# A gated linear attention and a squared-relu MLP on one core: block products in digit order, and a planner with new durations, a margin and new priorities

## The chip, the cores and the metric

The kernel runs on one core of a Trainium2 chip. The metric is the device time of one execution in microseconds; lower is better. A core has five engines that run side by side, each through its own list of instructions in a fixed order: TensorE (PE, with its weight loads PEld), VectorE (DVE), ScalarE (ACT), GpSimd (POOL) and SyncE (SP). SP and POOL here mostly issue DMA transfers. An instruction that isn't ready holds up everything behind it on its engine, whether that is ready or not.

## The reference

Four batches of 768 tokens, eight heads of 48 features. Each head has a complex state that decays by a per-token, per-feature factor and takes in k times v; the query reads its real part. The result is laid out as 3072 tokens by 384 features and goes through an MLP with 2048 hidden features.

```python
mag = np.sqrt(a_re * a_re + a_im * a_im)
scale = np.minimum(mag, 0.999) / (mag + 1e-06)
a_re_n, a_im_n = (a_re * scale, a_im * scale)
...
    new_re = ar * S_re - ai * S_im
    new_im = ar * S_im + ai * S_re
    kv = np.einsum('bhd,bhe->bhde', k[:, :, t], v[:, :, t])
...
h = x @ w_in
r = np.maximum(h, 0.0)
return (r * r @ w_out).astype(np.float32)
```

Here `kv` is the outer product of k and v of the token, added to `new_re`; the output is q times the real state.

## The kernel before

**Units.** The 3072 tokens are cut into six units of 512 (`NU` = 6). In a unit, a row of SBUF holds four neighbouring tokens, so that there are 128 groups of four. Each unit goes through three stages:

- `load` and `chain`: SP loads a, q, k and v. ACT and DVE normalise the decays (`roots`, `normalise`), multiply them up within each group of four (`inner`) and invert them (`inverse`). Then the running complex product over the 128 groups is formed. `totals` transposes the groups' totals on PE, so that features lie on partitions and groups along the row; ACT copies them into the tile `e`. `scan` forms the running product on DVE in three levels, each with a block of four or eight: within blocks of four groups, within blocks of four of those (tile `inc`), over the rest (tile `top`), and then back down. Each complex product in `product` is three DVE instructions (lines 989, 991, 993). The tile `x` takes a simpler real scan (line 963). `back` transposes the results on PE again (line 922), ACT copies them to `xn` (line 1055), and `apply` multiplies them into q and k on DVE (lines 1086 to 1104).
- `pairs`: per pair of heads, q and k are transposed, by PE and ACT in the first two units (`turn_pe`, lines 1186 and 1189) and by DVE and DMA later (`turn`, lines 1163 and 1167, into tiles `QT`). PE forms scores (line 1203), DVE masks them (line 1206), the states are kept (lines 1219 to 1237), and PE mixes (lines 1249 and 1253). ACT copies the result (line 1259) and SP moves it into `xT` (line 1267). `xT` has two slots, for even and odd units.
- `dense`: in two groups of 256 tokens, PE multiplies by w1 (line 1296), ACT applies relu and square (lines 1303 and 1304), PE multiplies by w2 (line 1314), ACT copies out (line 1318) and SP stores (line 1323). Twelve such groups in all.

**Weights.** They come as 64-bit words in sixteen pieces (`fetch` on POOL, line 728) and are converted by one ACT and three DVE instructions (`convert`, lines 738 to 747). The raw words are parked in tiles that are needed for other things later: raw w1 in the place of w2, in the g tiles and in a v tile; raw w2 in w2's free places, the v tile and the three QT tiles. So `pairs` of unit 1 has to wait for w2's raw words to leave QT. At the end `inspect` reads the weights once more and a check decides whether a general path has to run.

**Order.** The order isn't written out: every piece of work is entered as a step with an engine, an estimated duration, reads, writes and a rank. The class `Plan` then simulates the engines: it takes the engine that can start soonest and on it, among the steps that are ready at that time, the one of lowest rank. A step counts as ready after its inputs' ends plus `HOP` of their engine. The instructions are emitted in the order of the simulated start times, and that order is fixed on each engine on the chip. Ranks are pairs, compared left to right: pairs (1, unit), chain (2, unit), dense and weight conversion (3, ...), inspection (5, ...).

```python
def tt(n):
    return n / 960.0 + 0.07
...
CHAIN, PAIR, DENSE, CONV, LATE = 2, 1, 3, 3, 5
```

`tt`, `ts2` and `ac` estimate DVE, DVE fast forms and ACT from the elements per row; `dma` gives an issue time, a latency and a share of a bus.

## Time and profile before

| | us |
|---|---|
| median of 3 runs | 849.73 (849.67 to 854.43) |
| profiled execution, its own time | 850.27 |
| its span, first to last instruction | 848.5 |
| PE busy | 680.8 (80%) |
| PE weight loads busy | 517.5 (61%) |
| DVE busy | 516.5 (61%) |
| ACT busy | 339.3 (40%) |
| POOL busy | 78.2 (9%) |
| dense matmuls, line 1296, 1152 of 391 ns each | 268.6 |
| dense matmuls, line 1314, 768 of 494 ns each | 260.0 |

Matmuls overlap, so the sums by line run above the time that they take up: in the last 165 us a dense group takes 41.4. The page has a picture of the span in 40 slices of 21.2 us, each digit being the busy share in tenths, and PEclk the clock that TensorE was granted, in tenths of full speed:

```profile
PE   0117743199988999979879898987899999999994
DVE  5998899955588977799259995779656100000000
ACT  6632764133783435720088234661023131322220
PEclk9999977599999999989899999998899999999998
DMA  9803760372130266205490055501799200000001
```

DVE is nearly full in the first 200 us, in which the first two units' chains and the weights' conversion fall. PE is nearly full from there on, with dips at each unit's chain. From about 670 us only dense work is left and DVE is done.

### The profile page before, as it was taken

Reading aid. Unit: us, or ns where it says so; the run is one execution under the profiler, and the core shown is the slowest. Engines: PE = TensorE matmul, PEld = TensorE weight load, DVE = VectorE, ACT = ScalarE, POOL = GpSimd, SP = SyncE. Lnnn points to the kernel's source line nnn. Section 1 sums busy time; section 2 is a strip of 40 time slices with the busy share of each in tenths; the row PEclk is TensorE's granted clock in tenths of the full one; section 3 lists DMA queues with packets and bytes.
Section 4 is the critical chain, followed back from the end, with each engine's and each line's share of the span. In section 5 each row is a group of like instructions: output and inputs, shape, how many; then the busy total and the mean of one; then the engine's idle time right before and its main releaser. Section 6 shows DMA issues by size and latency. Waiting matters only on the chain.

```text
span 848.5 us, 10163 instructions
## 1 busy us (share of the span) xinstructions
PE 680.8 (80%) x3566; PEld 517.5 (61%) x3566; DVE 516.5 (61%) x978; ACT 339.3 (40%) x577; POOL 78.2 (9%) x154
## 2 busy tenths in 40 slices
PE   0117743199988999979879898987899999999994
PEld 0007633175875886756766596675687777777772
DVE  5998899955588977799259995779656100000000
ACT  6632764133783435720088234661023131322220
POOL 4000100010000220007000050003312000000000
PEclk9999977599999999989899999998899999999998
DMA  9803760372130266205490055501799200000001
GB/s 298 258 0 87 207 118 0 88 229 47 31 54 10 75 163 176 45 1 147 116 186 18 20 121 133 148 10 36 188 270 319 63 0 19 1 19 1 19 0 24
DMA packets 80509, 79.43 MB, mean 94 GB/s; under 512 B 35776, under 2 KB 65216, under 8 KB 80448
## 3 DMA queue, kind: packets, MB, share of 16 engines
q1 hardware_dynamic: 71488, 48.40, 23.7%
q0 software_dynamic: 8960, 30.29, 11.7%
q8 instruction: 30, 0.49, 0.3%
q14 instruction: 31, 0.25, 0.1%
HBM read 48.76 MB, written 4.72 MB: 63 GB/s over the span
## 4 chain that ended last, share of the span: by engine, by line
PE 42%; DVE 27%; SPq 8%; DMA 8%; ACT 6%; issue 4%; DVEq 0%; ACTq 0%; POOLq 0%
PE d L1314 18%; PE d L1296 17%; SPq L1167 5%; PE sc L1203 3%; DVE f L989 3%; DVE f L991 2%; DVE f L863 2%; DVE e L993 2%; DMA aq<-in_a_im_dram 2%; DMA QT<-aq 2%; DVE f L1091 2%; DVE f L1102 2%; DMA xT<-yt 1%; PE tr L1219 1%; DVE w L747 1%
## 5 line engine op out<-in xcount | busy, mean ns | idle before, releaser
L1296 PE MATMUL d<-xT,w 128*128 128x256 f32 x1152 | 268.6, 391 | 26.0 <-ACT g L1303 8.0
L1296 PEld LDWEIGHTS d<-xT,w 128*128 128x128 f32 x1152 | 222.7, 196 | 64.5 <-ACT g L1303 10.0
L1314 PE MATMUL d<-w,g 128*128 128x384 f32 x768 | 260.0, 494 | 1.5 <-DVE w L747 1.5
L1314 PEld LDWEIGHTS d<-w,g 128*128 128x128 f32 x768 | 146.0, 193 | 97.4 <-issue 4.5
L1303 ACT ACTIVATE g<-d 128x512 f32<-128x512 f32 x96 | 57.1, 595 | 138.0 <-PE d L1296 115.9
L1341 DVE TENSOR_SCALAR flag<-tr 1x1 int32<-1x1 f32 x1 | 0.1, 145 | 174.0 <-PE tr L1340 174.0
L1127 POOL DMA_DIRECT2D KC<-f x104 | 50.9, 498 | 375.8 <-DVE f L1102 188.1
L1203 PE MATMUL sc<-QT 96*128 96x128 f32 x384 | 52.2, 285 | 15.5 <-DMA QT<-aq 14.7
L1304 ACT ACTIVATE g<-g 128x512 f32<-128x512 f32 x96 | 60.6, 631 | 3.1
L1203 PEld LDWEIGHTS sc<-QT 96*128 96x128 f32 x384 | 48.6, 196 | 20.5 <-issue 15.4
L1318 ACT COPY ot<-d 128x384 f32<-128x384 f32 x24 | 11.5, 477 | 123.4 <-PE d L1314 120.2
L1206 DVE TENSOR_TENSOR A<-sc,mask 128x512 f32<-128x512 f32 x48 | 32.4, 686 | 39.8 <-PE sc L1203 39.8
L922 PE MATMUL tr<-ident,xn 128*128 128x128 f32 x54 | 10.3, 306 | 43.0 <-ACT xn L894 39.7
L1259 ACT COPY yt<-yp 112x512 f32<-112x512 f32 x24 | 13.9, 579 | 74.7 <-PE yp L1253 69.1
L1102 DVE TENSOR_TENSOR f<-aq 128x768 f32<-128x768 f32 x48 | 42.9, 954 | 0.4
L922 PE MATMUL tr<-ident,e 128*128 128x128 f32 x36 | 9.2, 427 | 42.1 <-DVE e L993 42.1
L1091 DVE TENSOR_TENSOR f<-aq,xn 128x768 f32<-128x768 f32 x48 | 42.5, 949 | 0.0
L1249 PE MATMUL yp<-A,v 128*48 128x128 f32 x384 | 37.8, 285 | 2.7 <-ACT yt L1259 2.0
L863 DVE TENSOR_TENSOR f<-aq 128x384 f32<-128x384 f32 x72 | 37.0, 555 | 1.0
L922 PEld LDWEIGHTS tr<-ident,xn 128*128 128x128 f32 x54 | 6.8, 152 | 46.7 <-issue 29.1
L1219 PEld LDWEIGHTS tr<-v,KC 128*96 128x96 f32 x320 | 31.9, 178 | 3.6 <-DMA xT<-yt 2.0
L922 PEld LDWEIGHTS tr<-ident,e 128*128 128x128 f32 x36 | 6.8, 218 | 44.6 <-DVE e L993 44.6
(143 smaller groups left out, 789.0 us busy)
## 6 DMA issues: line engine op xcount, KB each, us to landing
QT<-aq SPq DMA_DIRECT2D x192, 64.0 KB, 2.3
f<-in_moe_w_in_dram POOLq DMA_DIRECT2D x8, 768.0 KB, 8.8
f<-in_moe_w_out_dram POOLq DMA_DIRECT2D x8, 768.0 KB, 7.1
KC<-f POOLq DMA_DIRECT2D x104, 48.0 KB, 2.2
v<-in_v_dram SPq DMA_DIRECT2D x96, 48.0 KB, 2.5
out_dram<-ot SPq DMA_DIRECT2D x96, 48.0 KB, 1.6
xT<-yt SPq DMA_DIRECT2D x36, 96.0 KB, 3.7
aq<-in_a_re_dram SPq DMA_DIRECT2D x8, 384.0 KB, 3.8
```

Of the source, the lines that this page charges most:

```text
L863: dve.tensor_tensor(out=f, in0=a[:, :, :, c - 1], in1=a[:, j, :, c].unsqueeze(1).to_broadcast([C, 2, HH, D]), op=ALU.mult)
L1091: lambda j=j, f=f, r=r: dve.tensor_tensor(out=f[:, r], in0=a[:, r], in1=over(j), op=ALU.mult), rank)
L1102: lambda j=j, r=r, o=o: dve.tensor_tensor(out=o[:, :, :, r * D:(r + 1) * D], in0=qk[:, j], in1=a[:, r], op=ALU.mult), rank)
L1127: lambda i=i, c=c: queue.dma_start(out=kc[32 * c:32 * c + 32, i], in_=nat[32 * i:32 * i + 32, c]),
L1167: lambda b=b, j=j, z=z, t=t, T6=T6: sp.dma_start(out=t[32 * j:32 * j + 32, b], in_=T6[32 * b:32 * b + 32, i % 2, j]), rank, 65536,
L1203: pe.matmul(sa[:, j], lhsT=T[:, j, 1, h], rhs=T[:, j, 0, h], start=True, stop=True)
L1219: pe.matmul(ps[:, j, h], lhsT=kc[:, j, (2 * i + h) % HH], rhs=v5[:, j, 2 * i + h], start=True, stop=True)
L1249: pe.matmul(ypair[64 * h:64 * h + D, ts(j, C)], lhsT=v5[:, j, 2 * i + h], rhs=aa[h][:, j], start=True, stop=at[j] is None)
L1296: pe.matmul(ps[:, j], lhsT=w1[:, f // FP, m, ts(f % FP, C)], rhs=xT[:, m, base:base + G], start=(m == 0), stop=(m == NM - 1))
L1303: act.activation(out=o, in_=ps, func=AF.Relu)
L1304: act.activation(out=o, in_=o, func=AF.Square)
L1314: pe.matmul(ps, lhsT=gt[:, f % 2, ts(i, C)], rhs=w2[:, f], start=(f == 0), stop=(f == NF - 1))
```

## The change

It has five parts.

1. **Layout of the block products.** The 128 groups' index is read as three digits (k of 8, x of 4, w of 4). `e` is now laid out with w outermost, then x, then the feature block m and k; `inc` with x outermost. Every operand of a product of one level is then a run without gaps. To get there, `totals` transposes with a permutation matrix `perm` in place of the identity for the two complex parts, and writes PSUM in runs of eight (`spread`). The permutation also shifts by one group, so that ACT's copy to `e` is one run. `perm` is made by three POOL copies at the start. In `back` a new ACT copy per part puts `e` back into natural order before the transposes.
2. **Durations.** `HOP`, `ts2`, `ac`, the DMA issue time and latency and several steps' durations have other values.
3. **Margin.** In the plan, after 100 us, a PE step that depends on another engine or a DMA counts as ready 1.0 us later.
4. **Relu and output copy.** Their ACT steps have rank (0, unit): ahead of all others.
5. **Weight conversion.** w1's conversions have rank (2.5, piece), w2's (2, 0.6): behind the chain of unit 0, ahead of that of unit 1. The fetches keep their rank.

```diff
@@ -481,7 +481,8 @@
 class Plan:
 
 
-    HOP = {"PE": 0.12, "DVE": 0.1, "ACT": 0.15, "POOL": 0.2, "SP": 0.05}
+    HOP = {"PE": 0.3, "DVE": 0.17, "ACT": 0.1, "POOL": 0.2, "SP": 0.05}
+    MARGIN = 1.0
     RATE = 280e3
 
     def __init__(self):
@@ -530,7 +531,10 @@
             t = 0.0
             for d in steps[n][2]:
                 same = steps[d][0] == e and steps[d][5] is None
-                t = max(t, done[d] + (0.0 if same else self.HOP[steps[d][0]]))
+                hop = 0.0 if same else self.HOP[steps[d][0]]
+                if e == "PE" and not same and done[d] > 100.0:
+                    hop += self.MARGIN
+                t = max(t, done[d] + hop)
             at[n] = t
             wait[e].append(n)
 
...
@@ -653,6 +658,12 @@
     ypair = bank["yp"]
 
     make_identity(nc, ident)
+
+    turn_ = As[0][:, 0:C]
+    pool.tensor_copy(out=turn_[:, 1:C], in_=ident[:, 0:C - 1])
+    pool.tensor_copy(out=turn_[:, 0:1], in_=ident[:, C - 1:C])
+    pool.tensor_copy(out=perm.rearrange("p (w x k) -> p k x w", w=4, x=4),
+                     in_=turn_.rearrange("p (k x w) -> p k x w", w=4, x=4))
     pool.memset(mask, 1.0)
     for c in range(W):
         rows = mask[32 * c:32 * c + 32]
...
@@ -673,19 +684,20 @@
         return n / 960.0 + 0.07
 
     def ts2(n):
-        return n / 1920.0 + 0.08
+        return n / 1920.0 + 0.18
 
     def ac(n):
-        return n / 1200.0 + 0.12
+        return n / 1200.0 + 0.18
 
     def step(eng, dur, reads, writes, fn, rank, wire=None, group=None):
         return plan.add(eng, dur, reads, writes, fn, rank, wire, group)
 
-    def dma(q, reads, writes, fn, rank, size, lat=1.6, group=None):
-        step("SP" if q is sp else "POOL", 0.52 if q is sp else 0.8,
+    def dma(q, reads, writes, fn, rank, size, lat=1.8, group=None):
+        step("SP" if q is sp else "POOL", 0.6 if q is sp else 0.7,
              reads, writes, fn, rank, (lat, size), group)
 
     CHAIN, PAIR, DENSE, CONV, LATE = 2, 1, 3, 3, 5
+    W1, W2 = 2.5, 2
 
 
 
...
-        rank = (CONV, i)
+        rank = (W2, 0.6) if i >= NPIECE else (W1, i)
...
-        def turned(j, src, keys, name):
+        def turned(src, put, by, keys):
-            ps = bank[b][:, 0:DM].rearrange("p (m t) -> p m t", m=NM)
-                    pe.transpose(ps[:, m], src(m), ident)
+                    pe.transpose(put(bank[b][:, 0:DM], m), src(m), by)
             step("PE", 0.36, keys, [(b,)], go, rank)
-            return ps, (b,)
+            return bank[b][:, 0:DM], (b,)
+
+        def natural(t, m):
+            return t[:, ts(m, C)]
+
+        def spread(t, m):
+            return t.rearrange("p (y m k) -> p m y k", m=NM, k=8)[:, m]
 
...
-            ps, b = turned(j, lambda m: xn[:, j, ts(m, C)],
-                           [("xn", j, 0), ("xn", j, 1)], "tot")
+            keys = [("xn", j, 0), ("xn", j, 1)]
+            ps, b = turned(lambda m: xn[:, j, ts(m, C)], natural if j == 2 else spread,
+                           ident if j == 2 else perm, keys)
             if j < 2:
+                p4 = ps.rearrange("p (w g) -> p w g", w=4)
+                last = ps.rearrange("p (y m k) -> p y m k", m=NM, k=8)[:, 0, :, 0]
                 step("ACT", ac(DM), [b], [("e", j)], lambda: act.copy(
-                    out=e[:, j, :, 1:C], in_=ps[:, :, 0:C - 1]), rank)
+                    out=e[:, j], in_=p4), rank)
...
                     first = SCALE if j == 0 else 0.0
+                    head = e[:, j, 0].rearrange("p (x m k) -> p x m k", x=4, m=NM)[:, 0]
                     if fresh:
-                        dve.memset(e[:, j, :, 0], first)
+                        dve.memset(head[:, :, 0], first)
                     else:
-                        dve.tensor_copy(out=e[:, j, :, 0], in_=ce[:, j])
+                        dve.tensor_copy(out=head[:, :, 0], in_=ce[:, j])
                     if cross:
-                        dve.memset(e[:, j, :, CUT], first)
+                        dve.memset(head[:, :, 4], first)
...
-            v4 = e.rearrange("p r m (g w) -> p r (m g) w", w=4)
             for w in range(1, 4):
-                product(v4[:, 0:2, :, w], v4[:, 0:2, :, w - 1],
-                        lambda lo, hi, w=w: v4[:, lo:hi, :, w], 192, E, E)
-            i4 = inc.rearrange("p r (k w) -> p r k w", w=4)
+                product(e[:, 0:2, w], e[:, 0:2, w - 1], lambda lo, hi, w=w: e[:, lo:hi, w],
+                        192, E, E)
+            i4 = inc.rearrange("p r (x g) -> p r x g", x=4)
...
-                product(i4[:, 0:2, :, w], i4[:, 0:2, :, w - 1],
-                        lambda lo, hi, w=w: i4[:, lo:hi, :, w], 48, I, I)
+                product(i4[:, 0:2, w], i4[:, 0:2, w - 1], lambda lo, hi, w=w: i4[:, lo:hi, w],
+                        48, I, I)
...
-            x4 = incx.rearrange("p r (k w) -> p r k w", w=4)
-            product(x4[:, 0:2, :, 1:4], i4[:, 0:2, :, 0:3],
-                    lambda lo, hi: tx[:, lo:hi].unsqueeze(3).to_broadcast(
-                        [C, hi - lo, 24, 3]), 144, I, I)
+            step("DVE", 0.16, I, I, shift, rank)
+            x4 = incx.rearrange("p r (x g) -> p r x g", x=4)
+            product(x4[:, 0:2, 1:4], i4[:, 0:2, 0:3],
+                    lambda lo, hi: tx[:, lo:hi].unsqueeze(2).to_broadcast(
+                        [C, hi - lo, 3, 24]), 144, I, I)
...
-            product(v4[:, 0:2], v4[:, 0:2],
-                    lambda lo, hi: incx[:, lo:hi].unsqueeze(3).to_broadcast(
-                        [C, hi - lo, 96, 4]), 768, E + I, E)
+            step("DVE", 0.36, I, I, finish_inc, rank)
+            product(e[:, 0:2], e[:, 0:2],
+                    lambda lo, hi: incx[:, lo:hi].unsqueeze(2).to_broadcast(
+                        [C, hi - lo, 4, 96]), 768, E + I, E)
...
-            ps, b = turned(j, lambda m: x[:, m, 0:C] if j == 2 else e[:, j, m],
-                           [("x",) if j == 2 else ("e", j)], "bk")
+            if j == 2:
+                src, keys = (lambda m: x[:, m, 0:C]), [("x",)]
+            else:
+                line, keys = ff[0][:, Z + j * Y:Z + j * Y + DM], key(0, 2 + j)
+                step("ACT", ac(DM) + 0.2, [("e", j)], keys, lambda: act.copy(
+                    out=line.rearrange("p (g x w) -> p w x g", x=4, w=4),
+                    in_=e[:, j].rearrange("p w (x g) -> p w x g", x=4)), rank)
+                src = lambda m: line[:, ts(m, C)]
+            ps, b = turned(src, natural, ident, keys)
             step("ACT", ac(DM), [b], [("xn", j, 0), ("xn", j, 1)], lambda: act.copy(
-                out=xn[:, j], in_=ps.rearrange("p m t -> p (m t)")), rank)
+                out=xn[:, j], in_=ps), rank)
...
-            step("ACT", 2 * ac(2 * G), [(b, "x"), (b,)], [(b,), ("g", s)], relu, rank)
+            step("ACT", 2 * ac(2 * G), [(b, "x"), (b,)], [(b,), ("g", s)], relu, (0, n))
...
             step("ACT", ac(DM), [(b,)], [("ot", o)], lambda ps=ps, o=o: act.copy(
-                out=ots[o], in_=ps), rank)
+                out=ots[o], in_=ps), (0, n))
```

Left out are lines that carry the layout through (el, sums_of, tops, the last product) and the changed durations of single steps: inner +0.13, the scan of x 2.0 to 2.3, sums_of 0.45 to 0.5, tops 0.2 to 0.33, the sign change 0.09 to 0.12, shift 0.14 to 0.16, finish_inc 0.27 to 0.36, the state sums +0.04 each.

## The prediction

> **What bounds the kernel now.** I read the engine totals first, then TensorE's busy time by stage, then the waits on TensorE, then the order of instructions around the longest of them.
>
> ```profile
> 0.00:100.00 100.00, 33.08 (x282) 28.94 (x282) 84.22 (x161) 54.39 (x88) 11.16 (x30) 1.00 0.56 164
> 100.00:180.00 80.00, 36.39 (x170) 28.65 (x170) 73.20 (x140) 34.15 (x61) 3.52 (x5) 0.72 0.42 105
> 180.00:672.00 492.00, 446.50 (x2481) 339.26 (x2480) 358.89 (x677) 207.58 (x357) 63.57 (x120) 0.96 0.42 107
> 672.00:836.80 164.80, 164.80 (x639) 120.69 (x637) 0.00 (x0) 42.73 (x72) 0.00 (x0) 1.00 0.04 10
> 836.80:848.50 11.70, 0.01 (x1) 0.00 (x0) 0.14 (x1) 0.45 (x1) 0.00 (x0) 0.72 0.12 26
> ```
>
> The columns are stretch, length, busy time of PE, PE weight load, DVE, ACT and POOL, then granted clock. At 672 us DVE is finished and four dense groups are left, which PE does without a gap. So dense work is in stock from about 180 us to the end. What PE loses from there on is not for want of work. It is its own fixed order: it stands at an instruction that isn't ready while ready ones are queued behind. The idle of PE is 66.9 us before 100, 43.6 in 100 to 180, 45.5 in 180 to 672, and 11.7 at the end. The time is PE's work plus these four.
>
> ```profile
> PE tr L922 <- DVE e L993: 42.1, 6, 13.4
> PE sc L1203 <- DMA QT<-aq: 14.7, 12, 3.5
> PE d L1296 <- ACT g L1303: 8.0, 5, 3.1
> PE d L1296 <- DVE w L747: 7.8, 1, 7.8
> ACT QT L1189 <- DVE w L747: 8.2, 1, 8.2
> SPq L1323 <- ACT ot L1318: 235.3, 19, 29.2
> ```
>
> These are the waits: total, times, longest. Adding the single gaps of PE's timeline after 180 us gives: transposes of e on DVE's last product, 15.8 (3.59, 3.93, 3.88 and 4.36 in units 2 to 5); scores on the QT transfers, 14.7; dense matmuls on relu or on the output copy, 9.5; transposes of xn and x, 3.9; w, 1.5. The sum is 45.4, all of that stage.
>
> ```profile
> 372.27 1.54 PE L922 MATMUL tr<-ident,e 128*128 128x128 f32 x6 [3.93 <-DVE e L993]
> 373.60 4.86 PE L1296 MATMUL d<-xT,w 128*128 128x256 f32 x12
> 373.00:374.00 1.00, 1.00 (x5) 0.94 (x4) 1.00 (x2) 0.63 (x2) 0.00 (x0) 0.50 0.00 0
> 378.00:380.00 2.00, 2.00 (x9) 1.29 (x8) 1.97 (x3) 1.23 (x2) 0.00 (x0) 1.00 0.00 0
> ```
>
> The wait costs more than its length: after it the granted clock is 0.50, and twelve dense matmuls take 4.65 us before the next group starts, where the tail does 96 in 20.72 (2.59 for twelve).
>
> **The change part by part.**
>
> *Contiguous products.*
>
> ```profile
> L989 DVE TENSOR_TENSOR f<-e 128x192 f32<-128x192 f32 x18 | 9.0, 503 | 0.3
> L867 DVE TENSOR_TENSOR aq<-f 128x192 f32<-128x192 f32 x36 | 12.9, 358 | 1.2
> L989 DVE TENSOR_TENSOR f<-inc 128x48 f32<-128x48 f32 x18 | 4.4, 242 | 0.4
> ```
>
> The first and third read every fourth element, the second reads runs. Nine products of 192 per unit lose about 0.14 us each, nine of 48 about 0.035: 1.55 us per unit, 9.3 over six units.[...] In unit 1 the scan took 13.06 us (134.05 to 147.11 in the timeline), so about 11.5 after. This shortens DVE's chain, which doesn't set the end: four groups, 165 us, stand behind it.
>
> *The price of the layout.* Each unit gets two ACT copies that scatter e back. Row L1055 has a plain 128x384 copy at 476 ns; were ACT to lose on spread elements what DVE loses, 0.78. I take 0.65, so 7.8 us of ACT in all. Old path from scan to both xn copies in unit 3: 372.25 to 374.33, 2.1 us; new: 0.65 twice, transposes, copy, hops, 2.6. DVE has the two L1086 products and two of L1091 first and asks for the second xn only 3.9 us after the scan, so that hides it. If TensorE comes a dense step later (1.3), it is just met; without that cover DVE stalls about 1 us per unit, again in front of 165 us of stock.
>
> Six transposes per unit now write PSUM in runs of 8. In the trace the contiguous ones are 273 ns, pitch 0.137 (six in 0.82), and no PE row has a spread destination. Here a rule speaks against the change: the Trainium skill, "PSUM — Partial Sum Buffer", Specifications, says that any non-contiguous access pattern slows matmuls significantly. By the row the 36 transposes cost nothing more; by the rule, were it a doubling, 36 x 0.137 = 4.9 us. I take 0, because a run of 8 is nearer to the contiguous row, and keep 0 to 5; a gain is excluded. The three POOL copies at the start, near the 0.2 us memsets there, fall in POOL's idle time before the gate at 5.58.
>
> *Durations and margin.* The planner's old sum for unit 1's scan is 8.69 us (three products of 192 at 0.81, three of 48 at 0.36, the rest as in the code), 4.37 less than measured: that is the 3.6 to 4.4 us by which PE arrives early. With the new figures the plan has 9.04 for an actual 11.5: short by 2.5. The longer hop takes 0.07, the margin 1.0, leaving about 1.4 in each of four units: idle 15.8 to 5.6, gain 10.2.
>
> The slow clock goes with it. Excess over the normal pace after the four waits: 1.4, 2.8, 1.8, 2.0 (for unit 3: transposes 1.54 against 0.82, dense 4.65 against 2.59), sum 7.9. The Trainium skill, "TensorE: Matmul & The Clock Gate", What's actually happening, says that an idle window of some 3.4 us halves the clock and about as much activity restores it. By that rule each wait costs half of 3.4, 6.8 for four; I use the measured 7.9. More important, a gap of 1.4 lies below it, so I expect the whole 7.9 back.
>
> Waits of scores on QT: eleven of twelve are 0.45 to 1.47 us, one is 3.5. Margin 1.0, 0.2 more latency and 0.08 more for each of the DMA issues ahead cover the eleven and a part of the other: gain 12. The score runs at most one dense step later; queued behind it are DVE's mask products, which have idle time there (39.8 us behind scores). xn and x: 3 of 3.9.
>
> *Relu and output copy first on ACT.* The pair is 0.60 + 0.63 us and may now precede a ready chain step of 0.8 to 1.5. In 434 to 444 us PE waited 1.5, 3.1 and 0.6 behind chain work on ACT. Waits on an ACT that itself stands at a DMA stay. Gain 5 of 9.5, w another 1. The chain is pushed back by 1.2 us per collision, again in front of the stock. An earlier output copy frees SP earlier: its four stores (0.6 each) hold SP's queue, with QT transfers and loads behind them, but they are issued where the plan puts them.
>
> *w2 conversion ahead of the next chain.* One is an ACT step (0.89) and three DVE instructions, 0.55 + 0.96 + 0.96 = 2.47 us, and its end frees a slot for a POOL fetch of 768 KB (0.72 to issue, 7 to land), so two fetches move into 95 to 105 us, where the DMA share is already about 1 with chain 1's loads and xT on SP: at 300 GB/s some 5 us. Seven of the eight can go between 92 and 118 us: 17.3 us of DVE in front of chain 1, and w1's pieces 4 to 7 stay behind chain 1. PE, which waited until 168.1 for piece 5, would wait until about 181. Against it: pairs(1) stood until 201.97 because its QT slots held raw w2 (the ACT wait above), and now can run from about 170, some 10 us of PE work. Bounds: all 17 lost and 5 of DMA (+22), or pairs' 10 us and more filling old idle (-8). I take +4.
>
> *New waits.* A new order in all queues makes stalls that the trace can't show. Bound: nothing, or two of the old waits of 1.5 us in each of four units, 12. I take 6.
>
> **The sum.** 848.5 - 10.2 - 7.9 - 12 - 3 - 5 - 1 + 4 + 6 = 819.4. The profiled execution ran 1.8 us longer than its span (850.27), and the median of the runs, 849.73, is 0.5 below it: 821.
>
> **The rivals.** *Starved at the start (slower).* In 90 to 185 us, w2 before chain 1 holds back w1 pieces 4 to 7; PE idles at half clock, +22. For: DVE is 92% busy there, so each moved instruction moves the rest. Against: pairs(1) fills the hole. It decides the sign where the later stage returns less than 22; if that returns only 10, 849.7 + 12 = 862.
> *The margin just trades waits.* PE arrives in time at one step and late at the next, and the half clock stays where gaps stay above 3 us. Half of the 39, less 4 and 6: 849.7 - 9.5 = 840. For: planned errors of 2.5 us remain. If instead the order near the waits hardly alters, so that the change doesn't do what it says, only x, xn and small waits move: 847.
> *All of it.* Nearly all 45 of the stage and the 7.9 come back and the start gains 8, less 6 of stalls: about 800.
>
> **How the numbers follow.** Forecast 0.55 (810 to 832), all of it 0.12 (795 to 810), traded waits 0.13 (832 to 841), little change 0.11 (841 to 858), starved 0.09 (above 858). A measurement of this kernel can tell about 1% from no change, so faster, same and slower are 0.80, 0.11 and 0.09. The range 802 to 847 leaves out some 4% below and 14% above; the 5 us of PSUM writes lie within it.
>
> **What would show it.** Right: transposes of e wait below 2 us in units 2 to 5 with the clock at 1.00 after them; scores no longer wait on QT; products of 192 near 0.36 us; PE's idle in the middle near 20 us; pairs(1) starts near 170. Wrong: PE idle before 185 us above 125; spread transposes above 273 ns; PE at 0.5 in the middle; a dense stock below two groups when DVE ends.

## The result and the profile after

| | before | after |
|---|---|---|
| median of four runs, us | 851.97 (849.67 to 854.43) | 793.58 (788.41 to 794.33) |
| ratio, 95% interval | | 0.9301 (0.9248 to 0.9355) |
| profiled execution, its span | 850.27, 848.5 | 794.27, 792.5 |
| PE busy in the span | 680.8 | 672.1 |
| PE idle, 0 to 100 | 66.9 | 69.3 |
| PE idle, 100 to 180 ("early") | 43.6 | 18.8 |
| PE idle, 180 to 12 us before the end ("middle") | 45.5 | 21.9 |
| PE idle, the last 12 us | 11.7 | 10.4 |

The kernel is 7.0% faster, 58 us, where 29 were forecast. The spans differ by 56.0: 24.8 of idle time in the early stage, 23.6 in the middle, 1.3 at the end and 8.7 of busy time, less 2.4 lost before 100 us. The middle and the busy time came near what was forecast as sums; the early stage had been put down as a loss of 4.

Busy time of the kernel after in the two later stages, with the columns of the prediction's first fence:

```profile
100.00:180.00 80.00, 61.22 (x245) 45.45 (x246) 71.40 (x139) 49.79 (x86) 1.45 (x2) 0.82 0.39 89
180.00:625.00 445.00, 424.45 (x2335) 327.01 (x2334) 320.06 (x628) 213.14 (x367) 53.45 (x107) 0.98 0.36 90
```

From 100 to 180 us PE was busy for 36.39 us before and is for 61.22 now, at a granted clock of 0.82 instead of 0.72. DVE does no more there than before (71.40 against 73.20 us): it is the order of its work that changed. PE's waits of the kernel after (total, times, longest):

```profile
PE tr L933 <- ACT f L1079: 17.4, 4, 12.6
PE d L1325 <- DVE w L759: 8.1, 1, 8.1
PE sc L1232 <- DMA QT<-aq: 5.8, 5, 1.4
PE d L1325 <- ACT g L1332: 4.3, 2, 3.4
PE d L1325 <- ACT ot L1347: 3.4, 1, 3.4
```

The first row takes the place of the wait on e's last product; its 12.6 is unit 0's, before there is dense work. The other three are 4.8 together, where units 2 to 5 had lost 15.8. Scores wait for QT 5.8 instead of 14.7.

The step after a short wait, from PE's timeline of the kernel after (start, length, instruction, idle time before it):

```profile
486.21 0.55 PE L933 MATMUL tr<-ident,f 128*128 128x128 f32 x3 [2.17 <-ACT f L1079]
```

and the stretch behind it, from the busy times by window:

```profile
486.00:489.00 3.00, 2.79 (x16) 2.51 (x17) 1.76 (x3) 2.97 (x7) 0.00 (x0) 1.00 0.27 65
```

The gap of 2.17 us, the longest of the three, is followed by the full clock, where the gap of 3.93 before had been followed by 0.50. It isn't so after every short wait. Two other waits of the kernel after, each with a stretch behind it:

```profile
416.46 2.47 PE L1232 MATMUL sc<-QT 96*128 96x128 f32 x10 [1.36 <-DMA QT<-aq]
420.00:422.00 2.00, 2.00 (x11) 1.91 (x11) 0.51 (x2) 0.00 (x0) 0.00 (x0) 0.50 0.39 96
458.63 2.86 PE L1325 MATMUL d<-xT,w 128*128 128x256 f32 x12 [3.44 <-ACT g L1332]
460.00:462.00 2.00, 2.00 (x10) 1.55 (x10) 1.97 (x5) 0.34 (x1) 0.00 (x0) 1.00 0.03 8
```

After the wait of 1.36 the granted clock is 0.50 for some 10 us, though PE is busy without a gap; after the one of 3.44 it is 1.00. So the length of a wait alone doesn't tell what the clock does in this trace.

The groups of the new layout (busy time and mean ns of one):

```profile
L1079 ACT COPY f<-e 128x384 f32<-128x384 f32 x12 | 9.5, 852 | 24.0 <-DVE e L1015 24.0
L1011 DVE TENSOR_TENSOR f<-e 128x192 f32<-128x192 f32 x18 | 6.4, 356 | 0.5
L933 PE MATMUL tr<-perm,xn 128*128 128x128 f32 x36 | 5.9, 300 | 34.9 <-ACT xn L906 34.9
L933 PE MATMUL tr<-ident,xn 128*128 128x128 f32 x18 | 3.6, 304 | 2.8 <-ACT xn L909 2.8
```

Products of 192 fell from 503 to 356 ns, as the row of contiguous ones said. The scattering copy (the row of L1079) takes 0.85 us, not 0.65. A transpose that writes PSUM in runs of eight takes no longer than one that writes it in one run.

### Where the early gain sits

SP's timeline before, then after:

```profile
66.64 10.17 SPq L1127 DMA_DIRECT2D KC<-f  x16
76.92 1.39 SPq L792 DMA_DIRECT2D aq<-in_a_re_dram  x2
78.41 1.25 SPq L792 DMA_DIRECT2D aq<-in_a_im_dram  x2
79.77 10.83 SPq L1127 DMA_DIRECT2D KC<-f  x16
```

```profile
66.37 10.14 SPq L1156 DMA_DIRECT2D KC<-f  x16
76.61 0.72 SPq L804 DMA_DIRECT2D aq<-in_a_re_dram  x1
77.43 11.34 SPq L1156 DMA_DIRECT2D KC<-f  x16
90.08 0.66 SPq L804 DMA_DIRECT2D aq<-in_a_re_dram  x1
```

A gather of KC is 16 transfers that bring half of unit 0's k together for its states. Before, the four loads with which chain 1 begins were issued between the two gathers; after, only one of them, and the others from 90 us on. ACT started chain 1 at 83.75 before and at 100.35 after. In between DVE has no chain to serve and converts weights: the last piece of w1 ends at 154.8 instead of 173.0, and in DVE's timeline all of w2's but one by 126.3 instead of from 175 to 202. ACT's first step of chain 1 and DVE's last on w1, before and then after:

```profile
83.75 1.49 ACT L820 ACTIVATE f<-aq 128x1536 f32<-128x1536 f32 x1 [6.46 <-DMA aq<-in_a_im_dram]
172.03 0.96 DVE L747 CUSTOM_DVE_ANT_0 w<-v,w 128x1536 uint16<-128x1536 uint16 x1
```

```profile
100.35 1.48 ACT L832 ACTIVATE f<-aq 128x1536 f32<-128x1536 f32 x1 [11.49 <-DMA aq<-in_a_im_dram]
153.86 0.95 DVE L759 CUSTOM_DVE_ANT_0 w<-v,w 128x1536 uint16<-128x1536 uint16 x1
```

What PE then has, before and after:

```profile
147.17 1.54 PE L922 MATMUL tr<-ident,e 128*128 128x128 f32 x6 [12.92 <-DVE e L993]
158.41 1.91 PE L1186 MATMUL tr<-ident,f 128*96 128x128 f32 x8 [9.70 <-DVE f L1102]
168.12 10.46 PE L1296 MATMUL d<-xT,w 128*128 128x256 f32 x36 [7.80 <-DVE w L747]
```

```profile
120.42 15.05 PE L1325 MATMUL d<-xT,w 128*128 128x256 f32 x56 [4.22 <-DMA xT<-yt]
143.59 6.81 PE L1325 MATMUL d<-xT,w 128*128 128x256 f32 x24 [8.12 <-DVE w L759]
150.24 2.74 PE L1343 MATMUL d<-w,g 128*128 128x384 f32 x8
152.82 0.82 PE L933 MATMUL tr<-perm,xn 128*128 128x128 f32 x6
```

Before, PE stood for 30 us at three steps on chain 1 and on w1's later pieces. After, a w1 piece comes at 143.59, w2 is there already, and PE doesn't wait again until 267.84. Chain 1's scan comes 24 us later than before (its last product starts at 170.51 against 146.15 in DVE's timeline), and PE doesn't stand waiting for it.

### The profile page after: what moved, and what is told of

It is laid out like the page before. It is cut to its first block, busy times and chain, and to the rows that moved or that the text cites. A ratio compares the mean times of both kernels' runs of the same rounds, so it can differ in the third digit from the quotient of the medians.

```text
span 792.5 us, 10178 instructions
## 1 busy us (share of the span) xinstructions
PE 672.1 (85%) x3566; PEld 514.2 (65%) x3566; DVE 505.5 (64%) x978; ACT 346.3 (44%) x589; POOL 79.1 (10%) x157
## 4 chain that ended last, share of the span: by engine, by line
PE 37%; DVE 32%; DMA 9%; SPq 9%; ACT 5%; issue 3%; DVEq 0%; ACTq 0%
PE d L1325 14%; PE d L1343 14%; SPq L1196 5%; DVE f L875 4%; PE sc L1232 3%; DMA aq<-in_k_dram 3%; DVE f L1011 2%; DVE f L1131 2%; DMA xT<-yt 2%; DVE f L1013 2%; PE tr L1248 2%; DVE f L1120 2%; DVE aq L860 2%; DVE e L1015 2%; DMA QT<-aq 2%
## 5 line engine op out<-in xcount | busy, mean ns | idle before, releaser
L1325 PE MATMUL d<-xT,w 128*128 128x256 f32 x1152 | 265.4, 388 | 22.1 <-DVE w L759 8.1
L1343 PEld LDWEIGHTS d<-w,g 128*128 128x128 f32 x768 | 144.2, 191 | 91.8 <-issue 2.3
L1347 ACT COPY ot<-d 128x384 f32<-128x384 f32 x24 | 11.5, 477 | 102.4 <-PE d L1343 86.7
L1120 DVE TENSOR_TENSOR f<-aq,xn 128x768 f32<-128x768 f32 x48 | 42.6, 948 | 5.8 <-ACT xn L1084 5.8
L1278 PE MATMUL yp<-A,v 128*48 128x128 f32 x384 | 40.0, 292 | 2.7 <-DVE A L1235 2.6
L933 PE MATMUL tr<-perm,xn 128*128 128x128 f32 x36 | 5.9, 300 | 34.9 <-ACT xn L906 34.9
L1278 PEld LDWEIGHTS yp<-A,v 128*48 128x48 f32 x384 | 25.0, 130 | 12.8 <-issue 5.8
L1248 PE MATMUL tr<-v,KC 128*96 128x48 f32 x320 | 32.6, 260 | 0.0
L888 ACT ACTIVATE f<-aq 128x1536 f32<-128x1536 f32 x12 | 17.8, 1484 | 28.8 <-DVE aq L881 28.8
```

Source lines behind the costliest of these rows:

```text
L1120: lambda j=j, f=f, r=r: dve.tensor_tensor(out=f[:, r], in0=a[:, r], in1=over(j), op=ALU.mult), rank)
L1248: pe.matmul(ps[:, j, h], lhsT=kc[:, j, (2 * i + h) % HH], rhs=v5[:, j, 2 * i + h], start=True, stop=True)
L1278: pe.matmul(ypair[64 * h:64 * h + D, ts(j, C)], lhsT=v5[:, j, 2 * i + h], rhs=aa[h][:, j], start=True, stop=at[j] is None)
L1325: pe.matmul(ps[:, j], lhsT=w1[:, f // FP, m, ts(f % FP, C)], rhs=xT[:, m, base:base + G], start=(m == 0), stop=(m == NM - 1))
L1343: pe.matmul(ps, lhsT=gt[:, f % 2, ts(i, C)], rhs=w2[:, f], start=(f == 0), stop=(f == NF - 1))
```

## Experiments

All are against the kernel before, run beside it; "early" and "middle" are PE's idle time in the two stages, "busy" PE's busy time, in us, from one profile each. The kernel before ran anew beside each group of runs, with medians from 849.64 to 853.36 us, so small differences between runs are read from the ratios.

| run | time | ratio (95%) | early | middle | busy |
|---|---|---|---|---|---|
| before | 851.97 | 1 | 43.6 | 45.5 | 680.8 |
| after | 793.58 | 0.9301 (0.9248-0.9355) | 18.8 | 21.9 | 672.1 |
| e1 after, old conversion rank | 791.65 | 0.9294 (0.9251-0.9338) | 22.4 | 25.4 | 664.1 |
| e2 after, old relu rank | 820.61 | 0.9638 (0.9608-0.9668) | 22.1 | 40.2 | 678.1 |
| e3 after, no margin | 794.98 | 0.9358 (0.9312-0.9405) | 18.1 | 25.8 | 670.5 |
| e4 after, old durations | 834.12 | 0.9795 (0.9763-0.9827) | 41.1 | 29.3 | 684.9 |
| e5 before, layout alone | 843.85 | 0.9935 (0.9899-0.9970) | 39.9 | 41.3 | 683.6 |
| e6 after, old DMA figures | 825.36 | 0.9688 (0.9647-0.9730) | 34.0 | 29.5 | 684.2 |
| e7 after, old hops | 774.62 | 0.9096 (0.9059-0.9134) | 25.3 | 11.3 | 660.7 |
| e8 after, old ACT and fast DVE durations | 804.43 | 0.9448 (0.9410-0.9487) | 24.5 | 32.7 | 668.6 |
| e9 after, old DVE step durations | 789.99 | 0.9274 (0.9242-0.9306) | 19.8 | 27.4 | 666.5 |
| e10 before, new durations | 830.94 | 0.9765 (0.9749-0.9782) | 33.4 | 35.3 | 677.3 |
| e11 the same and relu rank | 812.17 | 0.9553 (0.9534-0.9572) | 35.0 | 25.9 | 671.5 |
| e12 the same and conversion rank | 802.39 | 0.9420 (0.9380-0.9461) | 26.4 | 26.3 | 670.9 |
| e14 after, chain 1's loads first | 806.28 | 0.9473 (0.9436-0.9511) | 28.0 | 24.0 | 674.8 |
| e15 before, chain 1's loads last | 841.46 | 0.9900 (0.9857-0.9942) | 37.2 | 41.0 | 680.1 |
| e16 after, old hops, no margin | 797.86 | 0.9388 (0.9342-0.9433) | 28.4 | 24.5 | 669.5 |
| e17 after, old hops, old DVE steps | 787.99 | 0.9258 (0.9224-0.9292) | 19.1 | 25.7 | 667.7 |
| e18 e15 and conversion rank | 860.86 | 1.0091 (1.0059-1.0122) | 41.2 | 46.0 | 696.0 |
| e19 e14 and old conversion rank | 803.13 | 0.9405 (0.9374-0.9436) | 25.6 | 23.5 | 673.2 |

### One part undone, and one alone

**e1**, the weight conversions back at their old rank:

```diff
-        rank = (W2, 0.6) if i >= NPIECE else (W1, i)
+        rank = (CONV, i)
```

> The changed kernel with the conversions of w1 and w2 back at their old rank (3, piece). In the changed kernel TensorE idles 18.8 us between 100 and 180 us where it idled 43.6 before. Theory A, that w2's conversions ahead of the second chain bring this: idle there back near 43, pairs of the second unit again stand until w2 has left the QT tiles, time near 818 us. Theory B, that relu's rank on ACT or the new durations bring it: idle there stays below 25, time 790 to 800. The prediction's step, that the early conversions cost 4 us: time near 789.

Nothing that can be told from the kernel after (the intervals overlap almost wholly), and 3.6 us more idle in the early stage. Chain 1 still starts late, and DVE now converts w1 first: its last piece ends at 102.3. Theory B's numbers came (idle below 25, time 790 to 800). Whether w1 or w2 fills the gap makes no difference that the time shows here, and the rank by itself is not the early gain.

**e2**, relu and output copy back at the dense rank:

```diff
-            ... relu, (0, n))
+            ... relu, rank)
-                out=ots[o], in_=ps), (0, n))
+                out=ots[o], in_=ps), rank)
```

> The changed kernel with relu and the output copy back at the dense rank (3, unit). The prediction gave this part 5 us: time near 799, with waits of dense matmuls on relu back at some 9 us. Theory B, that relu ahead of the chain on ACT holds the chain back and so opens DVE for w1's pieces 5 to 7: idle of TensorE between 100 and 180 us back above 35, time near 815. Theory A: idle there stays near 19, time 794 to 800.

It costs 27 us, more than either theory had, 18.3 of them idle time in the middle; the early stage stays at 22.1. PE's waits there, in the trace of e2 from 180 to 620 us:

```profile
PE d L1325 <- ACT ot L1347: 10.5, 2, 9.9
PE d L1325 <- ACT g L1332: 7.5, 2, 6.9
```

One output copy behind chain work holds PE for 9.9 us. In the kernel before all waits of this kind after 180 us were 9.5 together.

**e3**, no margin:

```diff
-    MARGIN = 1.0
+    MARGIN = 0.0
```

> The changed kernel with a margin of 0. By the prediction the margin's share is about 1 us in each wait on e in four units[...], and 8 of the 12 us of score waits: 12 to 16 us in the middle stage, time 806 to 810. If the new durations alone did the work: 794 to 798. The start, where the margin acts only after 100 us, should hardly differ.

The margin does what it says to the waits: transposes of e in units 1 to 5 wait 10.0 us without it (a row of 22.6, less unit 0's 12.6) and 4.8 with it, scores on QT 8.9 and 5.8. The middle has 3.9 us less idle with it. In the time nothing of this is to be measured: the intervals overlap, and the 12 to 16 us expected by the prediction did not come.

**e4**, all durations, hops and DMA figures as before; **e5**, the layout alone (e4 with e1, e2 and e3 as well).

> The changed kernel with all old durations, hops and DMA figures, but layout, margin and ranks as changed. By the prediction PE would arrive about 3 us early at e even with the margin (plan short by 4.4 less 1.55 of layout, less 1.0 of margin, plus a copy it counts right): waits near 2 us, time 800 to 805. Theory C, that durations bring the gain at the start: idle between 100 and 180 us back above 35 and time near 820.

> The kernel before with the layout alone: old durations, hops, ranks, no margin. The prediction counts nothing for it at the end of the span, but the plan's shortfall at e falls from 4.4 to about 2.7 us with the copy counted, so TensorE's waits on e fall below 3 us in four units, and the half clock after them mostly goes: 835 to 842. If the layout only moves DVE: 848 to 851. If the added ACT copies cost: above 853.

The durations are worth 41 us of the 58 when they are taken away last, and 22.3 of it is idle time in the early stage, as theory C had it. The layout alone is worth 0.65% (0.30 to 1.01), some 5 us, which lies between the two amounts expected.

### Which durations

```diff
# e6
-        step(..., 0.6 if q is sp else 0.7,      lat=1.8
+        step(..., 0.52 if q is sp else 0.8,     lat=1.6
# e7
-    HOP = {"PE": 0.3, "DVE": 0.17, "ACT": 0.1, ...
+    HOP = {"PE": 0.12, "DVE": 0.1, "ACT": 0.15, ...
# e8
-    ts2: n / 1920.0 + 0.18     ac: n / 1200.0 + 0.18
+    ts2: n / 1920.0 + 0.08     ac: n / 1200.0 + 0.12
# e9: the durations of DVE's single steps (2.3, 0.5, 0.33, 0.12, 0.16, 0.36, +0.13, +0.04)
#     back to (2.0, 0.45, 0.2, 0.09, 0.14, 0.27, 0, 0)
```

> The changed kernel with the old DMA issue times (0.52 and 0.8) and latency (1.6) alone. In all runs with the new figures SP issues only one load of the second chain before the second gather (line 1156 in the changed kernel) and the chain starts near 100 us, where before four loads come first and it starts at 83.75; the free DVE then converts w1. If the DMA figures do this and w1's supply sets the idle at the start: four loads first again, idle between 100 and 180 us above 33, time 808 to 820. If the order on SP returns but the idle does not: the supply is set elsewhere, 793 to 800.

> The changed kernel with the old hops alone (PE 0.12, DVE 0.1, ACT 0.15). If hops carry the 40 us that undoing all durations costs: 815 to 834. If the DMA figures or ACT's durations do: 791 to 799, since the margin of 1.0 covers the smaller hop.

> The changed kernel with the old estimates of ACT steps (n/1200 + 0.12 in place of 0.18) and of the quick DVE steps (n/1920 + 0.08 in place of 0.18) alone. A relu pair is then planned 0.12 us short. If those carry the gain: 815 to 834, with waits on relu. If not: 791 to 799.

> The changed kernel with the old durations of single DVE steps alone (products within groups without 0.13, the scan of x 2.0, the small ones, state sums). If DVE's steps decide the order at the start: idle of TensorE between 100 and 180 us back above 35, time near 818. If it is the DMA figures, the hops or ACT's durations: idle there below 25, time 793 to 803, with waits on e longer by about 1 us.

Three numbers for what it costs to issue and land a DMA carry 32 us, more than expected. With the old ones SP again issues chain 1's four loads between the gathers (76.47 and 77.97 in its timeline), and 15.2 us of early idle time come back. PE's waits of e6 show the rest:

```profile
PE sc L1232 <- DMA QT<-aq: 17.0, 10, 3.4
PE d L1325 <- DMA xT<-yt: 9.9, 1, 9.9
```

Scores wait 17.0 us for QT, 11.2 more than after, and busy time grows by 12 us at a lower clock. In the early stage the idle time came back, but not where the expectation had it. From e6: a row of PE's waits from 100 to 180 us, a line of PE's timeline and one of DVE's:

```profile
PE tr L933 <- ACT xn L906: 15.4, 2, 9.1
191.32 4.11 PE L1325 MATMUL d<-xT,w 128*128 128x256 f32 x12 [2.23 <-DVE w L759]
190.31 0.95 DVE L759 CUSTOM_DVE_ANT_0 w<-v,w 128x1536 uint16<-128x1536 uint16 x1
```

DVE converts w2 first and the last piece of w1 only at 191.3, behind chain 1, which is the order that the prediction had. But of the 34.0 us of early idle time 15.4 are spent at two transposes of chain 1 and 9.9 at xT, and only 0.6 on w; the wait on w1's last piece is 2.2 us. The old ACT durations cost 11 us, between the two sides of their expectation; the old DVE durations cost nothing that can be told; the old hops make the kernel 19 us *faster* than the change does. Neither side of e7's expectation had that. Whether or not the new hops describe the chip better, they don't lead to the better order.

### Parts added to the kernel before, one after the other

e10 has the new durations and hops, e11 also the relu rank, e12 also the conversion rank; the kernel after adds layout and margin.

> The kernel before with the new durations, hops and DMA figures alone: old layout, ranks, no margin. If durations carry 40 us by themselves, as undoing them in the changed kernel suggests: 808 to 815, with the idle of TensorE between 100 and 180 us near 20. If they work only together with relu's rank (or with the layout, whose products they describe): 830 to 845 and idle there above 35.

> The kernel before with the new durations and relu's and the output copy's rank; old layout, old conversion rank, no margin. If those two parts are the whole change: 790 to 798. If the layout is worth its DVE time too: 800 to 812, with waits on e near 2 us longer than in the changed kernel.

> The kernel before with the new durations, relu's rank and the conversion rank: the changed kernel without layout and margin. Without the conversion rank this stood at 812.2, with w2's pieces 2 to 7 converted only at 181 to 192 us and TensorE waiting for them. If w2's rank cures that: idle between 100 and 180 us from 35 to about 20, time near 797, and layout and margin are worth little. If the layout is what opens the start: idle there stays above 30, time 808 to 814.

The ratios go 0.9765, 0.9553, 0.9420, 0.9301. e10 came near its second side, e11 just beyond its slower one, and e12 stands between its two (26.4 us of early idle time where 20 or over 30 were named). Durations take 10.2 us off the early idle time, the relu rank nothing, the conversion rank 8.7, layout and margin 7.6. So the same rank that could be undone in e1 for nothing is worth 1.3% here. e1 is e11 with layout and margin: without the new rank these two are worth 2.6% (0.9553 to 0.9294), with it 1.2%. PE's waits of e10, then e11:

```profile
PE d L1296 <- ACT ot L1318: 8.4, 1, 8.4
PE d L1296 <- ACT g L1303: 5.0, 3, 2.9
```

```profile
PE d L1296 <- ACT g L1303: 1.6, 1, 1.6
PE d L1296 <- ACT ot L1318: 1.2, 2, 1.0
```

In e10 the longest wait of the middle is an output copy; the relu rank takes 10.6 of these two rows' 13.4 away.

### Is it the order of the loads?

In e6 the order changed together with all that the DMA figures change. e14 puts the old order into the kernel after, e15 the new one into the kernel before; e18 and e19 do the same together with the conversion rank.

```diff
# e14, in load
-  ... in_=src), rank, m * 3072,
+  ... in_=src), (0, n) if n == 1 and half == 0 and z == 0 else rank, m * 3072,
# e15, in load
-  dma(queue, [], [(name, z)],
+  dma(queue, [("KC", 1)] if n == 1 else [], [(name, z)],
# e18: e15 and
-        rank = (CONV, i)
+        rank = (2, 0.6) if i >= NPIECE else (2.5, i)
# e19: e14 and e1
```

> The kernel after, with one edit: the four loads of a_re and a_im that chain 1 begins with get rank 0, so SP issues them inside the first gather of KC, as early as the kernel before had them. Theory (the early gain comes from chain 1 starting late): chain 1 starts on ACT near 80 to 84 instead of 100.35, takes DVE ahead of the weight conversion (rank 2 against 2.5), the last piece of w1 is converted after 165 instead of 154.8, PE's idle time from 100 to 180 us rises from 18.8 to 33 to 40 us, and the whole is about 808 to 815 us. Rival (the early gain comes from the other new durations and from the conversion rank of w2, and the order of the loads is only a mark of it): idle from 100 to 180 stays below 23 us and the time stays within 788 to 798 us.

> The kernel before, with one edit: the planner lets the loads of unit 1 wait for the second gather of KC, so chain 1 starts late, with everything else as before. Theory: chain 1 starts on ACT near 98 to 103 instead of 83.75, DVE converts w1 from about 80 on, its last piece ends before 155 instead of at 173.0, PE's idle time from 100 to 180 us falls from 43.6 to 20 to 30 us, and the whole is 828 to 838 us, some 14 to 22 below before. Rival: w1 is early but PE's wait moves to the pairs of unit 1 or to w2, which here are converted at the old rank; idle from 100 to 300 us together stays within 5 us of 51.6 and the time within 845 to 856 us.

It is a cause, and not all of it. In e14 ACT starts chain 1 at 75.91 us, the last piece of w1 is converted by 187.2, 9.2 us of early idle time come back, and the time rises by 12.7; that is between what theory (33 to 40) and rival (below 23) gave. In e15 chain 1 starts at 100.42 and w1 is converted by 114 us, but only 6.4 us of idle time go; the time of 841.46 lies between theory and rival. PE's timeline of e15:

```profile
118.06 17.16 PE L1296 MATMUL d<-xT,w 128*128 128x256 f32 x68 [2.28 <-DMA xT<-yt]
169.41 1.91 PE L1186 MATMUL tr<-ident,f 128*96 128x128 f32 x8 [9.24 <-DVE f L1102]
179.12 7.47 PE L1314 MATMUL d<-w,g 128*128 128x384 f32 x16 [7.80 <-DVE w L747]
```

Its first matmuls by w1 run to 135 without a gap, as the theory had it. Then the wait moves on: to unit 1's pairs and to w2, the rival's two places. That led to e18, w2 ahead of the chain as well.

> The kernel before with two edits: the loads of unit 1 behind the second gather of KC, as in the run before, and the conversion ranks of the kernel after (w1 2.5, w2 2 and 0.6). With the loads alone the time fell by 8 us and PE then waited from 100 to 180 us for w2 (7.8 us) and for the pairs of unit 1 (9.2 us). Theory (the early gain needs both, a late chain so that w1 is converted early and w2 ahead of the rest of the chain): the wait for w2 is gone, idle from 100 to 180 us falls from 37.2 to 20 to 28 us, and the time is 828 to 836 us. Rival (the rest of the early gain is the relu ahead of chain work or the new durations): idle from 100 to 180 stays at 33 us or more and the time within 4 us of 841.5 us.

> The kernel after with both undone: chain 1's first loads ahead of the gathers and the conversions at the old rank (3, i). The old rank alone moved nothing that can be measured (791.65 us), the loads alone cost 12.7 us. Theory: both together bring most of the early loss back, idle from 100 to 180 us 34 to 42 us and the time 808 to 820 us. Rival: with the relu ahead of chain work the conversions come as early without the rank, and the time stays within 4 us of 806.3 us.

The theory failed in both. In e19 the time stays near e14's, as its rival had it. e18 fits neither side: it became 1.9% slower than e15 by the ratios, some 16 us, and PE's timeline of e18 says how:

```profile
144.44 5.04 PE L1296 MATMUL d<-xT,w 128*128 128x256 f32 x12 [4.51 <-DVE w L747]
179.56 3.66 PE L1186 MATMUL tr<-ident,f 128*96 128x128 f32 x16 [10.36 <-DVE f L1102]
191.64 7.94 PE L1296 MATMUL d<-xT,w 128*128 128x256 f32 x24 [3.94 <-DVE w L747]
```

Now w1's last pieces lie behind chain 1 again and PE gets to them at 191.64, and the granted clock in the early stage is 0.68, where e15 has 0.74. The kernel after has the same rank and as late a chain, and gets them into the chain's gaps; which of its other parts opens those gaps was not settled. In e19 the old rank gives 803.1 against e14's 806.3 us. The conversion rank thus brought 1.3% on e11, nothing on the kernel after, and cost 0.7% (intervals just touching) on e14 and 1.9% on e15. It has no price of its own. What it does depends on where chain 1, the relu and w1's pieces stand when it is applied.

### Do hops and margin have a price of their own?

e16 is e7 without margin, e17 is e7 with e9.

> The kernel after with the old hop times (PE 0.12, DVE 0.1, ACT 0.15 us) and no margin on TensorE. With the new hops the margin is worth nothing measurable (794.98 against 793.58). Theory (the hops and the margin do one job, slack between engines in the planner; with both away PE again runs into late operands in the middle stage): 785 to 800 us, idle from 180 us on 10 or more above the 20.6 us that the old hops with margin leave there. Rival (the margin does nothing with either set of hops, and what the hops change is which order the planner happens to fall into): within 5 us of 774.6 us.

> The kernel after with the old hops and the old single DVE durations together: each alone was faster than the kernel after (774.62 and 789.99 against 793.58 us). If the two gains were causes of their own they would add up: about 771 us. If they are jumps of the planner's order, as I think, the sum says nothing: anywhere from 772 to 800 us, and the likeliest is slower than 774.6.

With the old hops the margin is worth 23 us (774.62 against 797.86), as the theory had it, with the new ones nothing that can be measured. The old DVE durations cost 13 us on top of the old hops. e9's own gain, which the expectation took as given, lies within the intervals. What e7 has over the kernel after is 10.6 us less idle time in the middle and 11.5 us less busy time, against 6.5 us more idle in the early stage. Its busy times in the middle:

```profile
180.00:620.00 440.00, 431.15 (x2363) 331.61 (x2363) 315.49 (x615) 215.78 (x373) 46.59 (x94) 1.00 0.35 87
```

From 180 to 620 us PE is idle for 8.9 us, 2% of the stage, at a granted clock of 1.00. e7 is the fastest version here, in four runs between 773.99 and 774.68. Why these hops in particular meet the chip's own timing so well was not settled.

## Why the prediction was wrong, and where it was right

**The step that failed** is "w2 conversion ahead of the next chain", taken at +4 with bounds of +22 and -8. It was the sum's only term for the early stage, and that stage lost 24.8 us of idle time: these 28.8 us are about the whole of the error (the time came out 27 us below the forecast), and the other deviations nearly cancel. The term rested on "w1's pieces 4 to 7 stay behind chain 1" and on PE waiting for them until about 181, and so on chain 1 starting when it had started before. But the change also altered the figure for issuing a DMA, and what that does to SP's queue was put at nothing: the prediction used the new figures only for the scores' waits. With them the loads with which chain 1 begins fell behind the second gather and chain 1 started at 100.35 instead of 83.75. DVE converted w2 in the time in which the prediction had chain 1, and w1's last four pieces, ending at 106.9, 143.5, 146.8 and 154.8, fell inside chain 1 and not behind it. PE's wait on w ended at 143.59.

With chain 1's loads early the forecast order does appear: in e6 and e14 w1's last piece ends at 191.3 and 187.2. Even there the cost was misjudged, since the early stage has 34.0 and 28.0 us of idle time, less than the 43.6 before, and PE waits little on w. A late chain is not enough either: the kernel before with late loads and the new rank (e18) leaves w1's last pieces until 191.64. Of a planner's new duration every queue that it reorders should have been gone through, and SP's list at 77 us was one that mattered.

Of the 24.8 us, 15.2 go back with the DMA figures alone (e6) and 9.2 with the order of the loads alone (e14). How the rest divides stays open: with the parts added in turn it is 10.2 for the durations, 8.7 for the conversion rank and 7.6 for layout and margin, with 1.6 given back by the relu rank, but those shares hold only for that sequence.

**The middle stage** was right as a sum: 25.2 us of idle time forecast net, 23.6 measured. Not all of its terms were:

- *Transposes of e*: 10.2 forecast, 15.8 down to 4.8 measured, 11.0. The waits of 1.42, none, 2.17 and 1.18 stand where about 1.4 each were forecast. Right.
- *Scores on QT*: 14.7 to 2.7 forecast, 5.8 left. Too much by 3.1. The new DMA figures carry 11.2 of these waits (e6), the margin about 3.1 (e3).
- *Relu and output copy first*: 5 forecast, and undoing it costs 27 us in the kernel after (e2) and 18.8 in the other sequence (e10 to e11). I had sized it by the 9.5 us of such waits in the trace of before. That a wait is short before doesn't bound it: with scores and e better timed, PE stood 8.4 (e10) or 9.9 us (e2) at one output copy.
- *New waits*: 6 forecast as a loss in every case; one of 3.4 on the output copy, one of 3.4 on relu and 1.7 on a mask product are in the trace after.

**The clock**: 7.9 forecast, 8.7 of busy time measured, and that agreement is in part luck. The four slow stretches behind the waits on e are gone, as forecast: the clock is 1.00 after the gaps of 1.42, 2.17 and 1.18. But the prediction took a gap of 1.4 for too short to slow PE, and the trace after has the clock at 0.50 behind waits of scores of 1.36 (from 416 us), 1.44 (from 540) and 1.33 (from 632). So "PE at 0.5 in the middle", named as a sign of being wrong, did occur; the trace before has such stretches too, one behind a wait of 1.43 at 413.70. What sets them was not settled. An estimate from the granted clock of each microsecond (busy time times what is missing to 1.00) gives 18.3 us lost from 180 us to the last 12 us before and 13.4 after, and 6.5 and 8.4 in the early stage. So some 3 of the 8.7 us are the clock, and the rest is open.

**The layout**: contiguous products as forecast (356 ns for 358, and 206 for the 207 that follow from 242 less 35). The copy was mis-sized by 0.2 us, and its cover didn't hold: DVE now waits 5.8 us in all for `xn` (row L1120, 0.0 before), the 1 us per unit named for that case; that it cost the end nothing was not shown. For the spread transposes I took 0, against the rule of the Trainium skill, "PSUM — Partial Sum Buffer", Specifications, that non-contiguous patterns slow matmuls significantly. The trace decides: 300 ns against 304. The mark "above 273 ns" was passed by both forms alike and so says nothing. "Doesn't set the end" held as a size: alone the layout gave about 5 us.

**The marks**: PE's idle time in the middle is 21.9 where 20 were named, and one wait on e is 2.17 where all were to be below 2. Pairs of unit 1 started at 185.11, not near 170, and that cost nothing since PE had w1 and w2 to do, which I hadn't foreseen. The rival "all of it", about 800 us with 8 from the start, was the nearest; it too had the start gain at a third of its size.

## What to carry to other kernels

When an instruction order comes from a planner, a new duration is a change of order: list which instructions swap on every queue, the DMA-issuing ones first, before costing anything. A priority or a margin has no price of its own; the same edit was worth +1.3%, 0, -0.7% and -1.9% here, so measure it in the final combination and try its neighbours (one set of old hops was worth another 19 us). A short wait in the old trace doesn't bound what a priority is worth: the wait on an output copy was 1.5 us before and 8.4 in e10, where other waits had become shorter.

## What the runs showed of the hardware

- An ACT copy of 384 elements to scattered places (runs of one) takes 852 ns, against 474 to 476 in one run; 650 had been taken.
- TensorE transposes that write PSUM in runs of eight cost nothing measurable, 300 ns against 304; six in a row took 0.82 us, as contiguous ones did.
- The granted clock behind a wait of TensorE didn't follow the wait's length: 0.50 for some 10 us after one of 1.36 us, 1.00 after one of 3.44 us.
